# A circular-convolution and maxout kernel on one core: filter loaded in natural order and expanded by one-hot products, transposes in bf16, one group of transposes moved into the first MoE tile

## Chip, cores and metric

One core of a Trainium2 chip. The metric is the time of one execution on the device in microseconds; it is given as the median of the runs, with the lowest and highest.

## What is computed

For each of 8 sequences of 3072 tokens by 256 features, a real Fourier transform along the tokens is multiplied by a complex filter and transformed back; the result goes, token by token, through a maxout layer.

```python
X = np.fft.rfft(x, axis=1)                    # x: 8 x 3072 x 256
F = (filt_r + 1j * filt_i)[None, :, :]        # 1537 x 256
y = np.fft.irfft(X * F, n=3072, axis=1)
t = y.reshape(24576, 256)
out = np.maximum(t @ w1, t @ w2) @ w_out      # w1, w2: 256 x 1024, w_out: 1024 x 256
```

All inputs and the output are fp32; the kernel works in bf16 with fp32 sums.

## The kernel before

**The transform in stages.** 3072 tokens are 128 x 24. The forward transform is a product with the table C1 over the 128 (`f1`, or `first_s1` for batch 0), a change of layout, and a product with the table U over the 24 (px). The spectrum is multiplied by the filter F on VectorE (pq), and comes back through the tables VP and VQ (pz), a second change of layout, and the table G1 in `s4`. Batches 1 to 7 change layout by writing to DRAM and reading back (tiles ad, bt, zd, zr). Batch 0, which has nothing to hide such a trip under, does it by TensorE products with an identity (`first_t1`, `first_t2`).

**The filter tile F** has 128 partitions. A partition holds one of 12 frequency blocks, going up or going down; with padding these 24 fill a quadrant of 32. The two halves of a 64-partition group hold the same values for the real and imaginary part of X, and the two 64-partition groups hold different offsets. Before the change, `load_f` fills 12 partitions at a time, with a reversed row order for the blocks going down; `copy_f` doubles them with VectorE copies; `pad_f` writes zeros on SP; frequency 0 and the Nyquist row come by `load_f0` and `patch_f0` in fp32 and are put in by `fix_f`.

**The maxout part.** `moe_h` computes relu(t (w1 - w2)) (weights Wd), and `moe_o` adds t M with M = w2 w_out, which `prep_w` makes once. A MoE tile is 512 tokens, eight steps; there are 48 tiles.

**Order.** Each engine executes its instructions in the order in which the program emits them; there is no scheduler. The prologue (batch 0 up to `s4(0)`) is written out by hand. Then a loop over tiles and steps runs `moe_h`, `moe_o` and whatever a table `todo` holds for that step: the other batches' stages, set with `plan(step, fn, ...)`.

In the prologue's loop over eight groups g, each step does px and the products with F (`first_s2`), a t1 group two steps ahead, and pz with the Zt copy for the group before (`first_s3`). In steps 0, 2 and 4 the second half of the product with F is done on GpSimd, from a copy of px that ScalarE makes (tile xs).

**Queues and buffers.** DMAs that change the type go through POOL (GpSimd's queue): the filter, x, the weights, also the output. SP issues the rest. PSUM in the prologue is one pool `p2` of four buffers of 4 KB a partition, used in turn by every product there (pa, pt, px, pz, pg, pv, pw); afterwards it is `ps` (six of 2 KB) and `pso`.

The names used in the prediction: `xb` is x in bf16, `uu` the phases from which ScalarE's sine makes U, `At` and `Zt` the results before `first_t1` and `first_t2`, `zr` what `s4` reads, `py` the product of `s4`, `po` that of `moe_o`.

Of the kernel before, what the change touches and what calls it, by code (L numbers as in the profile page):

```python
# [8 lines left out]
FP32 = mybir.dt.float32  # L9
# [6 lines left out]
D = 256  # L16
HID = 1024
N1 = 128
N2 = 24
# [10 lines left out]
def kernel(  # L30
# [58 lines left out]
    def load_x(b, c):  # L89
        t_ = xpool.tile([128, 4, D], BF16, tag="xb", name="xb")  # L90
        src = x[b].rearrange("(p n) d -> p n d", n=N2)
        G.dma_start(out=t_, in_=src[:, 4 * c:4 * c + 4, :])  # L92
        xb[b, c] = t_


    def load_f(ri):
        f = (filt_r, filt_i)[ri]
        for c in range(2):
            src = bass.AP(f.tensor, f.offset + 16 * c * D, [[128 * D, J], [64 * D, 2], [1, 16 * D]])
            G.dma_start(out=F[64 * c:64 * c + 12, ri].rearrange("p b u d -> p b (u d)"), in_=src)  # L100
        for b in range(2):
            for c in range(2):
                row0 = 128 - 64 * b - 16 * c
                src = bass.AP(f.tensor, f.offset + row0 * D, [[128 * D, J], [-D, 16], [1, D]])
                G.dma_start(out=F[64 * c + 12:64 * c + 24, ri, b], in_=src)

    def copy_f(ri, c):
        if c == 0:
            V.tensor_copy(F[32:64, ri, :, 1:16], F[0:32, ri, :, 1:16])
        else:  # L110
            V.tensor_copy(F[96:128, ri], F[64:96, ri])

    Z0 = init.tile([8, 8 * D], BF16)
    V.memset(Z0, 0.0)

    def pad_f():
        for c in range(2):
            nc.sync.dma_start(out=F[64 * c + 24:64 * c + 32].rearrange("p r b (h u) d -> p (r b h) (u d)", h=2),
                              in_=Z0.rearrange("p (o x) -> p o x", o=1).to_broadcast([8, 8, 8 * D]))


    F0 = init.tile([64, 2, 2, D], FP32)

    def load_f0():
        for ri, f in enumerate((filt_r, filt_i)):
            for p0, n in ((0, J), (12, J), (24, 8), (32, J), (44, J), (56, 8)):
                if p0 % 32 != 12:
                    src = bass.AP(f.tensor, f.offset, [[128 * D, n], [96 * D, 2], [1, D]])
                else:
                    src = bass.AP(f.tensor, f.offset + 64 * D, [[128 * D, n], [-32 * D, 2], [1, D]])  # L130
                nc.sync.dma_start(out=F0[p0:p0 + n, ri], in_=src)

    def patch_f0():
        nc.sync.dma_start(out=F0[32:33, 1, 0], in_=filt_i[1536:1537, :])
        nc.sync.dma_start(out=F0[32:33, 0, 0], in_=filt_r[1536:1537, :])

    SW = init.tile([128, 128], BF16)
    e0 = init.tile([128, 2], FP32)
    zero = init.tile([128, 1], FP32)
    V.memset(zero, 0.0)  # L140
    pid = init.tile([128, 1], FP32)
    G.iota(pid, pattern=[[1, 1]], base=0, channel_multiplier=1,
# [14 lines left out]
    V.memset(I128, 0.0)  # L157
    V.memset(SW, 0.0)
    V.memset(U.rearrange("p t (q x) -> p t q x", q=2)[:, :, :, 24:32], 0.0)
    V.memset(VP[:, :, :, 48:64], 0.0)  # L160
    G.affine_select(out=I128, in_=I128, pattern=[[-1, 128]], compare_op=OP.not_equal,
                    fill=1.0, base=0, channel_multiplier=1)
    for c in range(2):
        for q in range(2):
            sl = SW[:, 64 * c + 32 * q:64 * c + 32 * q + 32]
            G.affine_select(out=sl, in_=sl, pattern=[[-1, 32]], compare_op=OP.not_equal,
                            fill=1.0 - 2.0 * q, base=-64 * c - 32 * (1 - q), channel_multiplier=1)


    load_f(0)  # L170
    load_f(1)
    for c in range(6):
        load_x(0, c)

# [18 lines left out]
    def tables_u():  # L193
# [53 lines left out]

        V.tensor_scalar(t1, pid, 32.0, None, OP.is_ge)
        V.tensor_scalar(t1, t1, -32.0, pid, OP.mult, OP.add)
        V.tensor_scalar(e0[:, 0:1], t1, 0.0, None, OP.is_equal)  # L250
        V.tensor_scalar(e0[:, 1:2], e0[:, 0:1], -1.0, 1.0, OP.mult, OP.add)
# [3 lines left out]
    def sines_u(uu, mk):  # L255
        Uv = U.rearrange("p t (q x) -> p t q x", q=2)
        for q in range(2):
            S.activation(U[:, :, 32 * q:32 * q + 24], uu[:, q].rearrange("p t r j -> p t (r j)"),
                         AF.Sin, bias=zero, scale=TWO_PI)
        for dr in range(2):  # L260
            S.activation(Uv[:, 0, :, 12 * dr:12 * dr + 12], uu[:, :, 0, dr], AF.Sin, bias=zero, scale=mk[:, dr:dr + 1])

# [6 lines left out]
    def tables_pe():  # L269
        pg = p2.tile([128, 128], FP32, tag="p2", name="pg")  # L270
        TE.matmul(pg, C1, I128, start=True, stop=True)
        S.activation(G1, pg, AF.Copy)
        for h in (1, 0):
            pv = p2.tile([128, 2, 8, 64], FP32, tag="p2", name="pv")
            for u in range(8):
                for c, b in QUADS:
                    TE.matmul(pv[64 * c:64 * c + 64, b, u, 0:48],
                              U[64 * b:64 * b + 48, 16 * h + 8 * (u // 4) + 4 * c + u % 4],
                              I128[64 * b:64 * b + 48, 64 * b:64 * b + 48], start=True, stop=True)
            S.activation(VP[:, 8 * h:8 * h + 8, 0, 0:48], pv[:, 0, :, 0:48], AF.Copy)  # L280
            V.tensor_copy(VP[:, 8 * h:8 * h + 8, 1, 0:48], pv[:, 1, :, 0:48])
        for h in (1, 0):
            pw = p2.tile([128, 2, 512], FP32, tag="p2", name="pw")
            for k in range(2):
                TE.matmul(pw[:, k], SW, VP[:, 8 * h + 4 * k:8 * h + 4 * k + 4], start=True, stop=True)
            E = S.activation if h else V.tensor_copy
            E(VQ[:, 8 * h:8 * h + 8].rearrange("p u b n -> p (u b n)"), pw.rearrange("p k n -> p (k n)"),
              *((AF.Copy,) if h else ()))

# [133 lines left out]
    def first_t1(g, E):  # L423
        pt = p2.tile([128, 2, 2, D], FP32, tag="p2", name="pt")
        t0 = 8 * (g // 2) + 2 * (g % 2)
        for c in range(2):
            for i in range(2):
                for dh in range(2):
                    a_ = Af[:, 3072 * dh:3072 * dh + 4096].rearrange("p (m k) -> p k m", k=64)
                    for b in range(2):  # L430
                        TE.matmul(pt[64 * b:64 * b + 64, c, i, 128 * dh:128 * dh + 128],
                                  a_[:, 2 * (t0 + 4 * c + i) + b], I128, start=True, stop=True)
        o = bt[0][0:ROWS, 8 * (g // 2):8 * (g // 2) + 8].rearrange("p (c u) d -> p c u d", c=2)[:, :, 2 * (g % 2):2 * (g % 2) + 2]
        evac(E, o, pt[0:ROWS])

# [6 lines left out]
    def first_s2(g, pool):  # L442
# [7 lines left out]
        for k in range(2):  # L450
            pq.append(pqpool.tile([128, 2, 2, D], BF16, tag="pq", name="pq"))
            E, src = V, px[:, k]
            if k == 1 and pool:
                E = G
                src = init.tile([128, 2, D], FP32, tag="xs", name="xs")
                S.activation(src[0:FROWS], px[0:FROWS, k], AF.Copy)
# [4 lines left out]

    def first_s3(g, pq, Zt):
        pz = p2.tile([128, 2, 512], FP32, tag="p2", name="pz")
# [12 lines left out]

    def first_t2(j, E, Zt):
        pt = p2.tile([128, 4, D], FP32, tag="p2", name="pt")
        for n in range(4):
            for dh in range(2):  # L480
                TE.matmul(pt[:, n, 128 * dh:128 * dh + 128], Zt[:, dh, :, 4 * j + n], I128, start=True, stop=True)
        evac(E, zr[0][:, 4 * j:4 * j + 4].rearrange("p n d -> p (n d)"), pt.rearrange("p n d -> p (n d)"))
# [62 lines left out]

    pad_f()
    load_f0()
    patch_f0()
    table_c()
    Af = init.tile([128, 7168], BF16, name="At")  # L550
    At = Af[:, 0:6144].rearrange("p (h a n k) -> p h a n k", h=2, a=2, n=N2)
# [6 lines left out]
    load_wo()  # L558
    copy_f(0, 0)
    copy_f(0, 1)  # L560
    first_s1(0)
    sines_u(uu, mk)
    Zt = init.tile([128, 2, 128, N2], BF16, tag="uz", name="Zt")
    first_s1(1)
    copy_f(1, 0)
    copy_f(1, 1)
    tables_pe()
    for c in range(2, 6):
        first_s1(c)
    fix_f()  # L570
    order = (4, 5, 6, 7, 2, 3, 1, 0)
    first_t1(4, S)
    first_t1(5, V)
    pend = None
    for n, g in enumerate(order):
        pq = first_s2(g, n in (0, 2, 4))
        if n + 2 < 8:
            first_t1(order[n + 2], S)
        if n in (1, 3, 5):
            prep_wd(n // 2, *wf)  # L580
        if pend:
            first_s3(*pend, Zt)
        pend = g, pq
    first_s3(*pend, Zt)
    zr[0] = zrpool.tile([128, N2, D], BF16, tag="zr", name="zr")
    for j in range(6):
        first_t2(j, (V, S)[j % 2], Zt)
    setup.close()
# [36 lines left out]

    plan(5, prep_w)
    plan_f1(1, spaced(0, 0.5, 12), 6)
# [61 lines left out]
```

## Time and profile before

| | us |
|---|---|
| median of 13 runs | 567.47 |
| lowest, highest | 565.84, 568.75 |
| profiled execution: time | 568.25 |
| profiled execution: span | 566.1 |
| first product on PE | 31.7 |
| first px of batch 0 | 47.24 |
| end of the last Zt copy | 71.19 |
| first py (`s4(0)`) | 77.48 |
| first po | 92.94 |

| engine | busy us | share of the span |
|---|---|---|
| PE | 504.3 | 89% |
| PEld | 349.8 | 62% |
| ACT | 335.1 | 59% |
| DVE | 322.0 | 57% |
| POOL | 82.8 | 15% |

PE is TensorE's products, PEld its weight loads (they overlap), DVE is VectorE, ACT ScalarE, POOL GpSimd, SP SyncE; POOLq and SPq are their DMA issues. A share is an average over the whole span, and the prologue and the tiles have different limits, so times of stages count for more here. The clock column of a stage is the TensorE clock granted, 1.00 being full; idle time can show as 1.00. A timeline row has start, length, engine, line, operation, output and inputs, count, and in brackets the idle time before it and what ended that.

### The profile page before, as it was taken

The numbers are of one execution on the slowest core, as the hardware profiler recorded it, in microseconds if no ns is written. First come the engines' busy times: TensorE is split into PE (matmuls) and PEld (weight loads), VectorE is DVE, ScalarE is ACT, GpSimd is POOL, SyncE is SP. The second block draws the span as 40 slices with busy tenths as digits, with TensorE's granted clock in tenths as the row PEclk, the third lists the DMA queues.
The fourth block names the chain that finished last, engine by engine and source line by source line (L and its number), as shares of the span: only waits on it lengthen the run. The fifth ranks groups of instructions, "written<-read, shape, count | busy, mean of one in ns | idle before, by whom it ended". The sixth has DMA issues, their size and how long they took to land.

```text
span 566.1 us, 12026 instructions
## 1 busy us (share of the span) xinstructions
PE 504.3 (89%) x5068; PEld 349.8 (62%) x5145; DVE 322.0 (57%) x418; ACT 335.1 (59%) x595; POOL 82.8 (15%) x133
## 2 busy tenths in 40 slices
PE   0057788999999999999999999998999999999996
PEld 0045555566666676667666766666666766677774
DVE  8354732693377447654777367733875488643432
ACT  1055667578568856785567546764667556645541
POOL 4564600110110021001100120011100000000000
PEclk9997569999999999999999999999999999999999
DMA  8998214877996797579946895759855953441111
GB/s 79 87 267 145 40 39 115 147 166 184 267 186 163 199 223 181 162 193 200 217 124 196 210 194 146 197 150 215 176 145 185 202 129 100 131 136 68 76 73 76
DMA packets 69882, 87.56 MB, mean 155 GB/s; under 512 B 4706, under 2 KB 50532, under 8 KB 68836
## 3 DMA queue, kind: packets, MB, share of 16 engines
q1 hardware_dynamic: 52052, 44.84, 37.3%
q0 software_dynamic: 17776, 41.95, 29.6%
q8 instruction: 40, 0.66, 0.5%
q14 instruction: 14, 0.11, 0.1%
HBM read 53.74 MB, written 47.19 MB: 178 GB/s over the span
## 4 chain that ended last, share of the span: by engine, by line
PE 38%; issue 27%; DMA 5%; POOL 2%; DVE 1%; ACT 0%; POOLq 0%; SPq 0%
PE po L533 14%; PE ph L508 12%; PE po L528 3%; DMA bt<-ad 3%; PE pz L378 2%; PE px L397 2%; PE pa L343 2%; DMA ad<-at 2%; PE py L492 2%; POOL out_dram L539 2%; DVE pq L402 1%; ACT at L344 0%; SPq L353 0%; POOLq L684 0%; POOL xb L92 0%
## 5 line engine op out<-in xcount | busy, mean ns | idle before, releaser
L513 ACT ACTIVATE gt<-ph 128x512 bf16<-128x512 f32 x307 | 182.2, 600 | 110.6 <-PE ph L508 108.8
L533 PE MATMUL po<-Wo,gt 128*128 128x256 bf16 x1536 | 229.8, 273 | 3.2
L533 PEld LDWEIGHTS <-gt 128*128 128x128 bf16 x1536 | 150.2, 98 | 57.6
L402 DVE TENSOR_TENSOR pq<-px,F 120x1024 bf16<-120x1024 f32 x112 | 131.7, 1218 | 24.7 <-PE px L397 24.0
L535 DVE COPY ot<-po 128x512 f32<-128x512 f32 x96 | 66.3, 690 | 110.5 <-PE po L533 109.9
L539 POOL DMA_DIRECT2D out_dram<-ot x48 | 25.8, 538 | 451.2 <-DVE ot L535 403.4
L382 ACT ACTIVATE zt<-pz 112x512 bf16<-112x512 f32 x112 | 60.8, 594 | 45.6 <-PE pz L378 40.6
L508 PEld LDWEIGHTS <-Wd 128*128 128x128 bf16 x768 | 70.3, 98 | 26.5 <-issue 12.5
L511 DVE TENSOR_SCALAR gt<-ph 128x512 bf16<-128x512 f32 x77 | 52.9, 687 | 35.8 <-PE ph L508 28.3
L344 ACT ACTIVATE at<-pa 128x512 bf16<-128x512 f32 x84 | 49.9, 603 | 8.6 <-PE pa L343 7.2
L418 PE MATMUL pa<-C,xb 128*128 128x128 bf16 x48 | 4.9, 281 | 31.9 <-DMA xb<-in_x_dram 31.9
L492 PE MATMUL py<-G,zr 128*128 128x128 bf16 x384 | 29.8, 219 | 1.9 <-ACT zr L440 1.1
L343 PE MATMUL pa<-xb,C 128*128 128x512 bf16 x83 | 31.5, 390 | 0.0
L92 POOL DMA_DIRECT2D xb<-in_x_dram x48 | 29.5, 624 | 5.0 <-PE pa L418 3.1
L378 PE MATMUL pz<-pq,VP 56*64 56x256 bf16 x448 | 28.7, 271 | 1.0 <-DVE pq L402 0.8
L492 PEld LDWEIGHTS <-zr 128*128 128x128 bf16 x384 | 24.8, 98 | 6.5 <-issue 3.3
L378 PE MATMUL pz<-pq,VQ 56*64 56x256 bf16 x448 | 28.0, 268 | 0.0
L397 PE MATMUL px<-bt,U 48*64 48x256 bf16 x448 | 23.7, 281 | 2.4 <-DMA bt<-ad 2.4
L418 PEld LDWEIGHTS <-xb 128*128 128x128 bf16 x48 | 4.4, 131 | 32.7 <-DMA xb<-in_x_dram 32.2
L420 ACT ACTIVATE At<-pa 128x1024 bf16<-128x1024 f32 x6 | 5.8, 1023 | 28.4 <-PE pa L418 28.4
L457 DVE TENSOR_TENSOR pq<-px,F 120x1024 bf16<-120x1024 f32 x13 | 15.3, 1219 | 6.0 <-PE px L447 6.0
L397 PEld LDWEIGHTS <-U 48*64 48x64 bf16 x448 | 8.3, 104 | 14.6 <-issue 11.8
(357 smaller groups left out, 575.3 us busy)
## 6 DMA issues: line engine op xcount, KB each, us to landing
out_dram<-ot POOLq DMA_DIRECT2D x48, 512.0 KB, 4.3
xb<-in_x_dram POOLq DMA_DIRECT2D x48, 256.0 KB, 7.2
ad<-at SPq DMA_DIRECT2D x42, 256.0 KB
bt<-ad SPq DMA_DIRECT2D x28, 384.0 KB
zd<-zt SPq DMA_DIRECT2D x56, 192.0 KB
zr<-zd SPq DMA_DIRECT2D x14, 768.0 KB
wf<-in_moe_w_dram POOLq DMA_DIRECT2D x2, 1024.0 KB, 7.4
F<-Z SPq DMA_DIRECT2D x2, 256.0 KB
```

The costliest lines, as they stand in the source:

```text
L343: TE.matmul(pa, C1, xb[b, c // 2][:, 2 * (c % 2):2 * (c % 2) + 2], start=True, stop=True)
L344: S.activation(at[:, 2 * (c % 2):2 * (c % 2) + 2], pa, AF.Copy)
L378: TE.matmul(pz[c][64 * k:64 * k + 64, i], W[64 * c:64 * c + 56, 2 * g + i, k], pq[k][64 * c:64 * c + 56, ri, i], start=(ri == 0), stop=(ri ...
L382: S.activation(zt[0:ROWS, c, o:o + 2], pz[c][0:ROWS], AF.Copy)
L397: TE.matmul(px[k][64 * c:64 * c + 64, i], U[64 * k:64 * k + 48, t_], bt_[64 * k:64 * k + 48, t_], start=True, stop=True)
L402: V.tensor_tensor(pq[k][0:FROWS], px[k][0:FROWS].rearrange("p (o i) d -> p o i d", o=1).to_broadcast([FROWS, 2, 2, D]), F[0:FROWS, :, k, 2 ...
L492: TE.matmul(py[:, n], zr[b][:, 4 * i + n, 128 * dc:128 * dc + 128], G1, start=True, stop=True)
L508: TE.matmul(ph, Wd[:, dc, 128 * j:128 * j + 128], y_[:, dc].rearrange("p a b -> p (a b)"), start=(dc == 0), stop=(dc == 1))
L511: V.tensor_scalar(gt[tt][:, j], ph, 0.0, None, OP.max)
L513: S.activation(gt[tt][:, j], ph, AF.Relu)
L533: TE.matmul(p_, g_[:, jj, 128 * n:128 * n + 128], Wo[:, jj], start=False, stop=(jj == 7))
L535: V.tensor_copy(ot[tt][:, n - 1:n + 1], po[tt])
```

## The change

- The filter is loaded as 96 partitions of 16 rows in natural order (`load_f`, one DMA each for the real and the imaginary part, into zr-pool buffers). Batch 0's x is issued ahead of it, and both ahead of the iotas on POOL.
- `expand_f` makes two row pairs of F at a time: 16 products with one-hot matrices Sel pick, reverse, double and place the blocks, and ScalarE copies the result from PSUM. It runs 16 times: eight for the real part and two for the imaginary part ahead of the prologue's loop, six in it. `copy_f` and `pad_f` are gone. Inside a quadrant the order of the 24 rows is changed, and U, SW, e0 and F0 with it.
- `first_t1`, `first_t2` and `tables_pe` use transposes with bf16 results instead of products with fp32 results. The eight t1 groups are now all ahead of the loop, copied by VectorE; VP is copied in one instruction.
- Of `first_t2` only group 0 stays in the prologue; groups 1 to 5 are planned at steps 0 to 4 of the tile loop. `prep_w` moves from step 5 to 7. Zt no longer shares memory with the phases; xs comes from another pool.

```diff
     def load_f(ri):
-        f = (filt_r, filt_i)[ri]
-        for c in range(2):
-            src = bass.AP(f.tensor, f.offset + 16 * c * D, [[128 * D, J], [64 * D, 2], [1, 16 * D]])
-            G.dma_start(out=F[64 * c:64 * c + 12, ri].rearrange("p b u d -> p b (u d)"), in_=src)
...
+        Fs[ri] = zrpool.tile([96, 16, D], BF16, tag="zr", name="Fs")
+        src = (filt_r, filt_i)[ri]
+        G.dma_start(out=Fs[ri], in_=src[0:1536].rearrange("(p u) d -> p u d", u=16))
+
+    def expand_f(g, ri, E):
+        pf = p2.tile([128, 2, 2, D], FP32, tag="p2", name="pf")
+        for b in range(2):
+            for i in range(2):
+                u = 2 * g + i
+                for c in range(2):
+                    for dr in range(2):
+                        m, o = 4 * b + c, u
+                        if dr:
+                            m, o = (7 - m, 16 - u) if u else (7 - m + c, 0)
+                        p0 = 64 * c + 32 * dr
+                        TE.matmul(pf[p0:p0 + 32, b, i], Sel[:, m], Fs[ri][:, o], start=True, stop=True)
+        evac(E, F[:, ri, :, 2 * g:2 * g + 2].rearrange("p b u d -> p b (u d)"), pf.rearrange("p b u d -> p b (u d)"))
...
+    for c in range(6):
+        load_x(0, c)
+    load_f(0)
+    load_f(1)
     pid = init.tile([128, 1], FP32)
     G.iota(pid, pattern=[[1, 1]], base=0, channel_multiplier=1,
...
-        pt = p2.tile([128, 4, D], FP32, tag="p2", name="pt")
+        pt = P.tile([128, 4, D], BF16, tag="p2" if P is p2 else "ps", name="pt")
         for n in range(4):
             for dh in range(2):
-                TE.matmul(pt[:, n, 128 * dh:128 * dh + 128], Zt[:, dh, :, 4 * j + n], I128, start=True, stop=True)
+                TE.transpose(pt[:, n, 128 * dh:128 * dh + 128], Zt[:, dh, :, 4 * j + n], I128)
...
-    copy_f(0, 0)
-    copy_f(0, 1)
-    first_s1(0)
+    for c in range(6):
+        first_s1(c)
     sines_u(uu, mk)
...
     order = (4, 5, 6, 7, 2, 3, 1, 0)
-    first_t1(4, S)
-    first_t1(5, V)
+    for g in order[:4]:
+        first_t1(g, V)
+    tables_pe()
+    for g in order[:4]:
+        expand_f(g, 0, S)
+    for g in order[4:]:
+        first_t1(g, V)
+    tables_q(1, S)
+    tables_q(0, V)
+    for g in order[4:]:
+        expand_f(g, 0, S)
     pend = None
+    expand_f(4, 1, S)
     for n, g in enumerate(order):
+        if n < 7:
+            expand_f(order[n + 1], 1, S)
+        if n == 6:
+            fix_f()
         pq = first_s2(g, n in (0, 2, 4))
-        if n + 2 < 8:
-            first_t1(order[n + 2], S)
...
-    for j in range(6):
-        first_t2(j, (V, S)[j % 2], Zt)
+    first_t2(0, V, p2)
...
-    plan(5, prep_w)
+    for j in range(1, 6):
+        plan(j - 1, first_t2, j, (S, V)[j % 2], ps)
+    plan(7, prep_w)
```

More of the change, by code (lines that the diff above doesn't have):

```diff
@@ L93, in load_x @@
         xb[b, c] = t_
+    Sel = init.tile([96, 8, 32], BF16)
+    Fs = {}
     def load_f(ri):
-        f = (filt_r, filt_i)[ri]
-        for c in range(2):
-            src = bass.AP(f.tensor, f.offset + 16 * c * D, [[128 * D, J], [64 * D, 2], [1, 16 * D]])
-            G.dma_start(out=F[64 * c:64 * c + 12, ri].rearrange("p b u d -> p b (u d)"), in_=src)
-        for b in range(2):
[L102 to L122, printed above, removed]
+        Fs[ri] = zrpool.tile([96, 16, D], BF16, tag="zr", name="Fs")
[3 more added lines that the diff above has]
+        pf = p2.tile([128, 2, 2, D], FP32, tag="p2", name="pf")
+        for b in range(2):
+            for i in range(2):
[8 more added lines that the diff above has]
+        evac(E, F[:, ri, :, 2 * g:2 * g + 2].rearrange("p b u d -> p b (u d)"), pf.rearrange("p b u d -> p b (u d)"))
+    F0 = zpool.tile([64, 2, 2, D], FP32, tag="zt", name="F0")
     def load_f0():
@@ L126, in load_f0 @@
             for p0, n in ((0, J), (12, J), (24, 8), (32, J), (44, J), (56, 8)):
-                if p0 % 32 != 12:
+                if p0 < 32:
                     src = bass.AP(f.tensor, f.offset, [[128 * D, n], [96 * D, 2], [1, D]])
@@ L133, in patch_f0 @@
     def patch_f0():
-        nc.sync.dma_start(out=F0[32:33, 1, 0], in_=filt_i[1536:1537, :])
-        nc.sync.dma_start(out=F0[32:33, 0, 0], in_=filt_r[1536:1537, :])
+        nc.sync.dma_start(out=F0[12:13, 1, 0], in_=filt_i[1536:1537, :])
+        nc.sync.dma_start(out=F0[12:13, 0, 0], in_=filt_r[1536:1537, :])
     SW = init.tile([128, 128], BF16)
@@ L158 @@
     V.memset(SW, 0.0)
+    V.memset(Sel, 0.0)
     V.memset(U.rearrange("p t (q x) -> p t q x", q=2)[:, :, :, 24:32], 0.0)
@@ L162 @@
                     fill=1.0, base=0, channel_multiplier=1)
[L163 to L173, printed above, removed]
+    for q in range(2):
+        sl = SW.rearrange("p (c x) -> p c x", x=32)[:, :, 12 * q:12 * q + 12]
+        G.affine_select(out=sl, in_=sl, pattern=[[-32, 4], [-1, 12]], compare_op=OP.not_equal,
+                        fill=1.0 - 2.0 * q, base=-12 * (1 - q), channel_multiplier=1)
+    sl = Sel[:, :, 0:24].rearrange("p m (q j) -> p m q j", q=2)
+    for q in range(2):
+        G.affine_select(out=sl[:, :, q], in_=sl[:, :, q], pattern=[[-1, 8], [-8, J]], compare_op=OP.not_equal,
+                        fill=1.0, base=0, channel_multiplier=1)
     def table_c():
@@ L246, in tables_u @@
         V.tensor_tensor(uu, uu, ru, OP.subtract)
-        V.tensor_scalar(t1, pid, 32.0, None, OP.is_ge)
-        V.tensor_scalar(t1, t1, -32.0, pid, OP.mult, OP.add)
-        V.tensor_scalar(e0[:, 0:1], t1, 0.0, None, OP.is_equal)
+        V.tensor_scalar(t1, pid, 12.0, None, OP.is_equal)
+        V.tensor_scalar(e0[:, 0:1], pid, 0.0, t1, OP.is_equal, OP.add)
         V.tensor_scalar(e0[:, 1:2], e0[:, 0:1], -1.0, 1.0, OP.mult, OP.add)
@@ L255, in sines_u @@
     def sines_u(uu, mk):
-        Uv = U.rearrange("p t (q x) -> p t q x", q=2)
+        Uv = U.rearrange("p t (r x) -> p t r x", r=2)
         for q in range(2):
-            S.activation(U[:, :, 32 * q:32 * q + 24], uu[:, q].rearrange("p t r j -> p t (r j)"),
-                         AF.Sin, bias=zero, scale=TWO_PI)
+            S.activation(Uv[:, :, :, 12 * q:12 * q + 12], uu[:, q], AF.Sin, bias=zero, scale=TWO_PI)
         for dr in range(2):
-            S.activation(Uv[:, 0, :, 12 * dr:12 * dr + 12], uu[:, :, 0, dr], AF.Sin, bias=zero, scale=mk[:, dr:dr + 1])
+            S.activation(Uv[:, 0, dr, 0:24].rearrange("p (q j) -> p q j", q=2), uu[:, :, 0, dr], AF.Sin, bias=zero,
+                         scale=mk[:, dr:dr + 1])
     def fix_f():
@@ L269, in tables_pe, with tables_q @@
     def tables_pe():
-        pg = p2.tile([128, 128], FP32, tag="p2", name="pg")
-        TE.matmul(pg, C1, I128, start=True, stop=True)
+        pg = p2.tile([128, 128], BF16, tag="p2", name="pg")
+        TE.transpose(pg, C1, I128)
         S.activation(G1, pg, AF.Copy)
[L273 to L288, printed above, removed]
+        pv = p2.tile([128, 2, 16, 64], BF16, tag="p2", name="pv")
+        for u in range(16):
+            for c, b in QUADS:
+                TE.transpose(pv[64 * c:64 * c + 64, b, u, 0:48],
+                             U[64 * b:64 * b + 48, 8 * (u // 4) + 4 * c + u % 4],
+                             I128[64 * b:64 * b + 48, 64 * b:64 * b + 48])
+        V.tensor_copy(VP[:, :, :, 0:48].rearrange("p u b n -> p b u n"), pv[:, :, :, 0:48])
+    def tables_q(h, E):
+        pw = p2.tile([128, 2, 512], FP32, tag="p2", name="pw")
+        for k in range(2):
+            TE.matmul(pw[:, k], SW, VP[:, 8 * h + 4 * k:8 * h + 4 * k + 4], start=True, stop=True)
+        evac(E, VQ[:, 8 * h:8 * h + 8].rearrange("p u b n -> p (u b n)"), pw.rearrange("p k n -> p (k n)"))
     def load_w():
@@ L423, in first_t1 @@
     def first_t1(g, E):
-        pt = p2.tile([128, 2, 2, D], FP32, tag="p2", name="pt")
+        pt = p2.tile([128, 2, 2, D], BF16, tag="p2", name="pt")
         t0 = 8 * (g // 2) + 2 * (g % 2)
@@ L430, in first_t1 @@
                     for b in range(2):
-                        TE.matmul(pt[64 * b:64 * b + 64, c, i, 128 * dh:128 * dh + 128],
-                                  a_[:, 2 * (t0 + 4 * c + i) + b], I128, start=True, stop=True)
+                        TE.transpose(pt[64 * b:64 * b + 64, c, i, 128 * dh:128 * dh + 128],
+                                     a_[:, 2 * (t0 + 4 * c + i) + b], I128)
         o = bt[0][0:ROWS, 8 * (g // 2):8 * (g // 2) + 8].rearrange("p (c u) d -> p c u d", c=2)[:, :, 2 * (g % 2):2 * (g % 2) + 2]
-        evac(E, o, pt[0:ROWS])
+        evac(E, o.rearrange("p c u d -> p c (u d)"), pt[0:ROWS].rearrange("p c u d -> p c (u d)"))
     def evac(E, out_, in_):
@@ L454, in first_s2 @@
                 E = G
-                src = init.tile([128, 2, D], FP32, tag="xs", name="xs")
+                src = apool.tile([128, 2, D], FP32, tag="at", name="xs")
                 S.activation(src[0:FROWS], px[0:FROWS, k], AF.Copy)
@@ L460, in first_s2, with first_s3 @@
         return pq
-    def first_s3(g, pq, Zt):
+    def first_s3(g, pq):
         pz = p2.tile([128, 2, 512], FP32, tag="p2", name="pz")
@@ L475, in first_s3, with first_t2 @@
         S.activation(z, pz[:, :, 0:384].rearrange("p c (h m) -> p c h m", h=2), AF.Copy)
-    def first_t2(j, E, Zt):
-        pt = p2.tile([128, 4, D], FP32, tag="p2", name="pt")
+    def first_t2(j, E, P):
+        pt = P.tile([128, 4, D], BF16, tag="p2" if P is p2 else "ps", name="pt")
         for n in range(4):
             for dh in range(2):
-                TE.matmul(pt[:, n, 128 * dh:128 * dh + 128], Zt[:, dh, :, 4 * j + n], I128, start=True, stop=True)
+                TE.transpose(pt[:, n, 128 * dh:128 * dh + 128], Zt[:, dh, :, 4 * j + n], I128)
         evac(E, zr[0][:, 4 * j:4 * j + 4].rearrange("p n d -> p (n d)"), pt.rearrange("p n d -> p (n d)"))
@@ L544, in drain @@
             pass
-    pad_f()
     load_f0()
@@ L549 @@
     table_c()
+    Zt = late.tile([128, 2, 128, N2], BF16, name="Zt")
     Af = init.tile([128, 7168], BF16, name="At")
@@ L558 @@
     load_wo()
-    copy_f(0, 0)
-    copy_f(0, 1)
-    first_s1(0)
+    for c in range(6):
+        first_s1(c)
     sines_u(uu, mk)
[L563 to L566, printed above, removed]
+    order = (4, 5, 6, 7, 2, 3, 1, 0)
+    for g in order[:4]:
+        first_t1(g, V)
     tables_pe()
[L568 to L571, printed above, removed]
-    first_t1(4, S)
-    first_t1(5, V)
+    for g in order[:4]:
[6 more added lines that the diff above has]
+        expand_f(g, 0, S)
     pend = None
+    expand_f(4, 1, S)
     for n, g in enumerate(order):
+        if n < 7:
+            expand_f(order[n + 1], 1, S)
+        if n == 6:
+            fix_f()
         pq = first_s2(g, n in (0, 2, 4))
-        if n + 2 < 8:
-            first_t1(order[n + 2], S)
         if n in (1, 3, 5):
@@ L581 @@
         if pend:
-            first_s3(*pend, Zt)
+            first_s3(*pend)
         pend = g, pq
-    first_s3(*pend, Zt)
+    first_s3(*pend)
     zr[0] = zrpool.tile([128, N2, D], BF16, tag="zr", name="zr")
-    for j in range(6):
-        first_t2(j, (V, S)[j % 2], Zt)
+    first_t2(0, V, p2)
     setup.close()
```

## Prediction

> **What bounds the kernel now.** I read the stages first: the busy time of each engine in the stretches that the prologue falls into (columns: stretch and length, then busy us and count of PE, PEld, DVE, ACT, POOL, then granted clock, DMA share, GB/s).
>
> ```profile
> 0.00:31.70 31.70, 0.00 (x0) 0.00 (x0) 18.17 (x60) 2.28 (x5) 16.08 (x33) 1.00 0.93 92
> 31.70:47.24 15.54, 9.99 (x148) 8.21 (x150) 6.89 (x9) 11.02 (x15) 8.75 (x10) 0.93 1.08 271
> 47.24:71.24 24.00, 18.43 (x416) 13.62 (x416) 16.34 (x14) 13.76 (x17) 14.10 (x9) 0.57 0.43 67
> 71.24:77.48 6.24, 5.13 (x49) 5.08 (x49) 3.67 (x3) 3.07 (x3) 0.00 (x0) 0.63 0.01 3
> 77.48:92.94 15.46, 12.90 (x76) 6.68 (x78) 2.08 (x3) 12.49 (x25) 0.00 (x0) 0.89 0.23 85
> 92.94:566.10 473.16, 457.86 (x4381) 316.23 (x4453) 274.82 (x331) 292.42 (x531) 43.91 (x82) 1.00 0.68 164
> ```
>
> From 92.9 us PE is busy 97% of the time: its stream sets the end, and nothing there is edited. What counts is when that stream starts. For 31.7 us PE does nothing while the DMA engines are 93% busy at only 92 GB/s. The waits of that time say why:
>
> ```profile
> PEld L418 <- DMA xb<-in_x_dram: 32.2, 2, 31.7
> POOL F L105 <- DMA F<-in_filt_r_dram: 13.0, 3, 9.9
> DVE F L109 <- DMA F<-in_filt_r_dram: 7.7, 1, 7.7
> ```
>
> The first `first_s1` matmul waits for x; x's loads are issued on POOL behind twelve filter loads, and POOL's ninth filter load waits 9.9 us for an earlier one. The timeline has the x issues at 24.84. In the loop (47.24 to 71.24) I read one pair of steps:
>
> ```profile
> 58.67 0.64 PE L447 MATMUL px<-bt,U 48*64 48x256 bf16 x8
> 59.36 1.22 DVE L457 TENSOR_TENSOR pq<-px,F 120x1024 bf16<-120x1024 f32 x1 [0.71 <-PE px L447]
> 60.68 0.60 ACT L456 ACTIVATE xs<-px 120x512 f32<-120x512 f32 x1 [1.09 <-DVE pq L457]
> 61.35 2.14 POOL L457 TENSOR_TENSOR pq<-xs,F 120x1024 bf16<-120x1024 f32 x1 [1.08 <-ACT xs L456]
> 63.54 0.61 PEld L470 LDWEIGHTS <-pq 56*128 56x128 bf16 x28 [0.46 <-POOL pq L457]
> 64.22 0.64 PE L447 MATMUL px<-bt,U 48*64 48x256 bf16 x8
> ```
>
> A chain px, DVE product, ACT copy, POOL product, pz, next px, 5.55 us for two steps; no engine is full. PE ran there at about half clock (0.57).
>
> **What the skill says.** (1) *TensorE: Matmul & The Clock Gate*, "Part 3": small-M products with outputs in different 32-column groups run at once, 2.38x for three. The trace shows it for two groups only: 16 `first_t1` products (128 rows, 64 columns) take 1.05 us, 65 ns each, at half clock. No run here has four groups with 96 rows. (2) *VectorE: DVE Perf Modes*, "Why PSUM operands drop a tier": a PSUM source allows the two-fold mode for 16-bit, none for fp32. The fp32 half agrees: 1225 ns for 1024 elements. By it a bf16 PSUM copy would take an estimated 0.7 us; not shown before. (3) *DMA: Bandwidth & Descriptors*, "Why a DMA increments its semaphore by 16 and not by 1": a load over 96 partitions uses 16 engines, over 12 fewer. The filter's 92 GB/s against the 207 to 213 of x agrees in direction. (4) The first page again, "Part 4: PE-mode transpose": transposes do not count as busy for the clock; no run here shows it yet.
>
> **Part by part.** A: to the first product of the loop (before: 48.32).
> - POOL now issues six x loads and two filter loads first: 8 x 0.59 us (the row of x's issues) = 4.7, from 0.84, so the iotas start at 5.6, not 0.84. No wait ahead of them: before, eight loads were in flight before POOL stopped. Queued behind them on POOL are the iotas and selects, and DVE's table chain waits for those: it started at 2.57, now about 6.2. Shift 3.7: C1 done at 8.8 (5.1), `uu` at 17.7, DVE free at 18.4.
> - x is 6 x 262 KB as bf16; at 210 GB/s 7.5 us, landed by about 11. The filter halves, 0.79 MB each, add 3.7 us each: about 15 and 19, before their first use. The weights and batch 1, issued later on POOL, have until 60.
> - `first_s1`: from 8.8, a first product group of 1.0, then six ACT copies of 1.0: 15.9. `first_t1` x4: 4 x 1.05, PE done at 20.1; DVE copies from 18.4, 0.7 to 1.23 each, done at 21.3 to 23.3. `sines_u` 2.5 from 17.7: 20.2. The C1 and U transposes, 1.5: 21.7.
> - Then PE's order is four expansions, four t1, pw, four expansions, two more, px. One expansion is 16 products of 256 columns: at half clock a 512-column product took 0.43, so 256 take 0.21; four at once give 16 x 0.21/4 = 0.85, say 0.9. Bounds: 0.45 at full clock, 3.4 if none overlap. PE cold: 10 x 0.9 + 4 x 1.05 + 4 x 0.43 + 1 for switches = 16, and px 0.64: first product at 38.4. PE warm, ACT binds: one G1 copy 0.26, ten F copies and one VQ at 1.02 = 11.5, after a first expansion 0.9: 34.2. I take 36.3: **-12.0** (-14.1 to -9.9).
> - Gone: DVE's F copies (8.9 us) and SP's padding writes; both lay beside the wait for x and are worth nothing alone. Transposes stream as many columns as the identity products did; I price them alike (0.8 to 1.2 of it moves A by under 1 us). The VP copies become one, 0.9 to 1.7 us, hidden under the first expansions. The F0 loads on SP stay and are needed only at step 6 of the loop.
>
> B: the loop. 22.9 us from the first product to the last Zt. The t1 groups leave PE and ACT, an expansion and its F copy take their place. But every second expansion now stands between pz and the next px, on the chain shown: 3 x (0.9 + 0.38 for the switch of shapes that the timeline has as "issue") = 3.8 cold, 2.1 warm: **+3.0**. The other expansions lie under POOL's 2.14. `fix_f` (1.09 on DVE) moves ahead of step 6's products; DVE idled 0.67 there and the late px gives the rest: 0; up to +1.1 without it.
>
> C: last Zt to first py, 6.24. Now one group of 8 transposes (0.86), a drain of 0.2 and a DVE copy of 0.75 to 1.23: 2.0 to 2.3. **-4.2**.
>
> D: tile 0 gets 40 transposes: 4.3 us at half clock, 2.2 at full, and two ACT copies of 1.02, three on DVE, which idles. ACT is busy without a pause from 79.3 to 90, so neither engine hides it whole: steps 0 to 2 cold, 3 x 0.86, then one ACT copy 1.0: **+3.5** (1.5 to 5). `prep_w` from step 5 to 7: M is wanted at step 8, so PE has less beside its 0.69 copy: **+0.3** (-0.4 to +1).
>
> Sum: -12.0 + 3.0 - 4.2 + 3.5 + 0.3 = -9.4. The profiled execution took 568.25 (span 566.1, 2.15 around it), 0.8 above the median 567.47; 568.25 - 9.4 = 558.85, less 0.8: **558.0**.
>
> **Rivals.**
> R1, PE warms up: the expansions fill the array densely from 22 on, and the clock was seen rising to 1.0 at about 48.5 after dense groups. Then A is -14.1, B +2.1, C -4.2, D +2.5: -13.7, 553.8. Against it: the loop stayed at half clock from 52 on with PE nearly always busy, and t1 now consists of transposes.
> R2, slower: the expansion's 32-column products overlap less than four-fold. PE is the bound of A, ten expansions before px and three on the loop's chain, 13 in all: it decides from 0.9 + 9.4/13 = 1.6 us an expansion. Two at once, 1.75: +11, 569; none, 3.4: +32, 590. For it: no four groups shown. Against: two groups overlap fully.
> R3, little gain: x lands late because eight big loads and SP's small ones share the engines, or tile 0 pays all 4.3 and ACT's 2.0: about -3, 564.5. For: the first filter load took 15 us to land. Against: it was of narrow loads.
> That the change does not do what it says (x still behind the filter) is excluded by POOL's order.
>
> **How the numbers follow.** Main case 0.58 (own range 555.5 to 561.5), R1 0.18, R2 0.14, R3 0.10. A difference of 0.2%, 1.1 us, is about what can be told from none. Main, R1 and most of R3 are faster: 0.84; R2 with a warmer clock or R3 at its worst could end level: 0.03; slower 0.13. Range 552.5 to 565.5: it leaves out R2 and a tail of R1.
>
> **What would show it.** First L412 product at about 9, first px at 34 to 38, expansions of 0.5 to 0.9 us for 16, loop some 26 us, first py near 64, tile 0 some 19 us to the first po, then the same 473. Wrong if an expansion takes over 1.6 us, if x lands after 15, or if the stream after tile 0 lengthens by over 2 us.

## The result and the profile after

563.40 us median of 11 runs (562.30 to 566.17) against 567.64 of the kernel before: a ratio of 0.9933, 95% interval 0.9914 to 0.9951. So 4.2 us are gained, where 9.4 were forecast. All ratios below are to the kernel before, too. The profiled execution took 564.22, its span is 562.4.

The stages of the kernel after, in the columns used before (stretch and length, busy us of PE, PEld, DVE, ACT, POOL, clock, DMA, GB/s). They are cut at the first product on PE, the first product with F, the last Zt copy, the first py, the first po and the issue of the last store:

```profile
0.00:9.22 9.22, 0.00 (x0) 0.10 (x1) 3.60 (x19) 2.28 (x5) 8.12 (x26) 1.00 0.78 142
9.22:35.56 26.34, 23.22 (x428) 20.00 (x429) 16.28 (x49) 17.73 (x22) 4.27 (x8) 0.87 1.07 241
35.56:62.46 26.90, 15.82 (x392) 9.36 (x391) 17.77 (x16) 14.76 (x18) 14.04 (x9) 0.56 0.14 22
62.46:64.37 1.91, 1.08 (x8) 0.83 (x9) 0.69 (x1) 0.00 (x0) 0.00 (x0) 0.50 0.00 0
64.37:84.33 19.96, 16.62 (x116) 10.19 (x119) 4.15 (x6) 15.39 (x29) 0.00 (x0) 0.87 0.28 96
84.33:552.81 468.48, 457.85 (x4380) 316.26 (x4453) 274.84 (x331) 291.35 (x529) 43.37 (x81) 1.00 0.68 163
552.81:562.40 9.59, 0.00 (x0) 0.00 (x0) 0.00 (x0) 0.00 (x0) 0.53 (x1) 0.57 0.14 55
```

The last two stretches of the kernel before, for comparison:

```profile
92.94:561.67 468.73, 457.86 (x4381) 316.23 (x4453) 274.82 (x331) 292.42 (x531) 43.38 (x82) 1.00 0.68 164
561.67:566.10 4.43, 0.00 (x0) 0.00 (x0) 0.00 (x0) 0.00 (x0) 0.53 (x1) 0.76 0.29 118
```

The surprise stands in the last line of each. The first po comes 8.6 us earlier and the stream up to the last store takes the same 468 us, so that store is issued 8.9 us earlier. But from its issue to the end it is now 9.6 us, not 4.4, with every engine idle. The store is not the reason: its data have landed 2.9 us after the issue in both, and SP is through at 556.1. What is late is GpSimd's DRAIN, an instruction at the end of its program. Here are its rows in the view of the program's last line (min, median and max ns, then first and last start). The longest of the three is the first: it begins with the last store's issue, and in all traces here it ends only after that store has landed. After and before:

```profile
L682 POOLq DRAIN  x3: 51/93/8873, 552.8 to 562.2; - x3
```

```profile
L684 POOLq DRAIN  x3: 51/102/3649, 561.6 to 565.8; - x3
```

It lasts 8.87 us instead of 3.65, and 5.2 of the 8.9 us are lost in it.

The waits of the first 100 us, after:

```profile
PE pa L412 <- ACT C L188: 9.2, 1, 9.2
PEld L412 <- DMA xb<-in_x_dram: 5.7, 1, 5.7
```

x is there at 5.7; PE now waits for the table C1, which was made to wait behind the DMA issues on POOL, until 9.2. And the pair of steps of the loop, after (timeline):

```profile
41.32 0.64 PE L441 MATMUL px<-bt,U 48*64 48x256 bf16 x8
42.09 1.22 DVE L451 TENSOR_TENSOR pq<-px,F 120x1024 bf16<-120x1024 f32 x1 [3.04 <-PE px L441]
...
43.34 0.60 ACT L450 ACTIVATE xs<-px 120x512 f32<-120x512 f32 x1 [0.88 <-DVE pq L451]
...
44.02 2.12 POOL L451 TENSOR_TENSOR pq<-xs,F 120x1024 bf16<-120x1024 f32 x1 [2.42 <-ACT xs L450]
...
46.20 0.61 PEld L464 LDWEIGHTS <-pq 56*128 56x128 bf16 x28 [1.88 <-POOL pq L451]
...
46.87 1.05 PE L115 MATMUL pf<-Fs,Sel 96*32 96x256 bf16 x16
...
47.85 0.64 PE L441 MATMUL px<-bt,U 48*64 48x256 bf16 x8
```

The chain is the old one with the expansion as a new link before px: 6.53 us from px to px, 0.98 more than before.

### The profile page after: what moved, and what is told of

The parts are those of the page before. It is cut to its first block, busy times and chain, and to the rows that moved or that the text cites. A ratio compares the mean times of both kernels' runs of the same rounds, so it can differ in the third digit from the quotient of the medians.

```text
span 562.4 us, 12527 instructions
## 1 busy us (share of the span) xinstructions
PE 514.6 (91%) x5324; PEld 356.7 (63%) x5401; DVE 317.3 (56%) x420; ACT 341.5 (61%) x601; POOL 70.3 (13%) x123
## 3 DMA queue, kind: packets, MB, share of 16 engines
q0 software_dynamic: 15632, 41.95, 28.2%
## 4 chain that ended last, share of the span: by engine, by line
PE 48%; issue 18%; DMA 5%; DVE 2%; POOL 1%; ACT 0%; POOLq 0%; SPq 0%
PE po L527 18%; PE ph L502 16%; PE po L522 4%; DMA bt<-ad 3%; PE pz L372 3%; PE px L391 3%; PE pa L337 2%; PE py L486 2%; DMA ad<-at 2%; DVE pq L396 1%; POOL out_dram L533 1%; ACT at L338 0%; SPq L347 0%; DVE ot L529 0%; DVE gt L505 0%
## 5 line engine op out<-in xcount | busy, mean ns | idle before, releaser
L396 DVE TENSOR_TENSOR pq<-px,F 120x1024 bf16<-120x1024 f32 x112 | 131.7, 1218 | 24.5 <-PE px L391 23.7
L486 PEld LDWEIGHTS <-zr 128*128 128x128 bf16 x384 | 25.1, 99 | 6.8 <-issue 3.4
L92 POOL DMA_DIRECT2D xb<-in_x_dram x48 | 26.2, 554 | 10.1 <-DMA Fs<-in_filt_i_dram 3.9
L391 PE MATMUL px<-bt,U 48*64 48x256 bf16 x448 | 23.7, 281 | 2.2 <-DMA bt<-ad 2.2
L434 ACT ACTIVATE F<-pf 128x1024 bf16<-128x1024 f32 x16 | 15.5, 1031 | 2.5 <-PE pf L115 2.5
L464 PE MATMUL pz<-VP,pq 56*128 56x48 bf16 x128 | 6.9, 213 | 10.2 <-POOL pq L451 6.1
L372 PEld LDWEIGHTS <-VP 56*64 56x64 bf16 x448 | 13.2, 106 | 3.1 <-DVE pq L396 1.6
```

The lines of the kernel that those rows point to most:

```text
L372: TE.matmul(pz[c][64 * k:64 * k + 64, i], W[64 * c:64 * c + 56, 2 * g + i, k], pq[k][64 * c:64 * c + 56, ri, i], start=(ri == 0), stop=(ri ...
L391: TE.matmul(px[k][64 * c:64 * c + 64, i], U[64 * k:64 * k + 48, t_], bt_[64 * k:64 * k + 48, t_], start=True, stop=True)
L396: V.tensor_tensor(pq[k][0:FROWS], px[k][0:FROWS].rearrange("p (o i) d -> p o i d", o=1).to_broadcast([FROWS, 2, 2, D]), F[0:FROWS, :, k, 2 ...
L486: TE.matmul(py[:, n], zr[b][:, 4 * i + n, 128 * dc:128 * dc + 128], G1, start=True, stop=True)
```

## The experiments

**The last drain.** GpSimd issues 101 DMAs after and 111 before, and the profile's packets on its queue are 15632 and 17776. A packet here is one contiguous piece that a DMA moves: d_desc's six loads, in four pieces a partition instead of one, add 6 x 384. The first four runs ask whether one of these counts decides it. In d_split10 (and d_split5) ten (five) late x loads are halved; in d_desc six take four packets a partition; f_fix7 leaves the DMAs as they are.

```diff
+        if 6 * b + c >= 38:            # d_split5: 43
+            for p in (0, 64):
+                G.dma_start(out=t_[p:p + 64], in_=src[p:p + 64, 4 * c:4 * c + 4, :])
```

> The changed kernel, with ten late x loads (the last four of batch 6, all of batch 7) issued as two loads of 64 partitions each: 111 POOL loads and stores as in the kernel before, instead of 101, but almost the same number of DMA packets (15632 + 160). Theory D1 (GpSimd's last drain grows with how few DMAs it has issued, whatever their size): the last drain goes from 8.87 us to about 3.65, the time falls by about 5 us to 558. Theory D2 (it depends on the number of packets in the descriptor rings, 15632 against 17776): the drain stays near 8.5, the time near 563. Theory D3 (it has to do with what is issued at the start, x ahead of the iotas): stays 8.9.

> As d_split10, with five x loads halved: 106 POOL DMAs, 15712 packets. D1, if the drain is linear in the count: about 6.3 us and a time of 561; if it is a step, 8.9 or 3.7. D2 and D3: 8.8 and 563.

```diff
+        if b == 7:
+            G.dma_start(out=t_, in_=bass.AP(x.tensor, x.offset + (b * N + 4 * c + 3) * D, [[N2 * D, 128], [-D, 4], [1, D]]))
```

> The changed kernel, with the six x loads of batch 7 reading their four rows in reverse, so that each partition takes four packets instead of one (the last batch is computed from reordered tokens): still 101 POOL DMAs, but 15632 + 2304 = 17936 packets, near the 17776 of the kernel before. D1: drain stays 8.9 us, time 563 to 564. D2: drain about 3.5, time about 558. D3: 8.9.

Measured (last drain, then time): d_desc 3.71 us, 559.55 us (ratio 0.9857, 0.9818 to 0.9897). d_split10 9.69 us, 564.03 (0.9953, 0.9939 to 0.9966); d_split5 9.28 us, 563.44. D1 fell, in direction too: more DMAs make the drain longer, by 0.082 us each. D3 fell with d_desc. D2 is right that packets decide between short and long, but not how: 160 more packets did not shorten it a little. The other kernels here with 101 DMAs and 15632 packets (f_fix7, and t2_back and x_after_f further down) have 8.87, like the kernel after.

For d_split10's 0.82 us I first blamed its 160 packets, which gives a saw tooth of 5.1 ns a packet. The next runs add packets without DMAs: some stores turn their four rows round and so write four pieces a partition.

```diff
+        rev = 6 <= tt < 7              # o_rev2: 8, o_rev9: 15, best6: 12
+        p_ = po[tt][:, 1 - n % 2 if rev else n % 2]
...
+            if rev:
+                o = bass.AP(out.tensor, out.offset + (b * N + 4 * i + 3) * D, [[N2 * D, 128], [-D, 4], [1, D]])
```

> The changed kernel, with the store of MoE tile 6 in four packets a partition instead of one (its four rows are kept in reverse on the chip and turned round by the store): 15632 + 384 = 16016 packets. So far the drain was 8.87, 9.28, 9.69 us at 15632, 15712, 15792 packets, 5.1 ns a packet, and 3.65 and 3.71 at 17776 and 17936. Theory S (a saw tooth: it grows by 5.1 ns a packet and falls to its floor where the descriptor ring wraps, somewhere between): 8.87 + 384 x 0.0051 = 10.8 us here, if the wrap lies above 16016, else about 3.7. Theory H (a hump or a step with another cause, such as the size of the packets): 8.9.

> As o_rev1 for tiles 6 and 7: 16400 packets. Theory S with a wrap at 1024 packets for each of the 16 engines, 16384: 3.7 us. Theory S with a wrap above 16400: 12.8 us. Theory H: 8.9.

> As o_rev1 for tiles 6 to 14: 15632 + 9 x 384 = 19088 packets, well past the count of the kernel before. Theory S: the tooth grows again, so the drain is longer than 3.7, by 5.1 ns for every packet past the point where it leaves the floor; if the tooth starts at 16384, (19088 - 16384) x 0.0051 = 13.9 us. Theory H: about 3.7, as at 17776 and 17936.

Measured, in one execution each: last drains of 8.87, 3.31 and 4.02 us. The tooth is refuted, and H, which had 8.9 for o_rev2, did not hold either: 384 pieces more change nothing (o_rev1), the next 384 take 5.6 us away (o_rev2), and 2688 more add 0.7. The step lies between 16016 and 16400, and what adds 0.082 us below it is the DMA, not the packet. The profile still counts 15632 packets in these runs, so the number of pieces is worked out; that GpSimd makes more of them shows in the issue of such a store, 0.75 to 0.78 us against 0.53.

If that is a rule of the queue and not of this kernel, it must work on the kernel before:

```diff
-                src = bass.AP(f.tensor, f.offset + row0 * D, [[128 * D, J], [-D, 16], [1, D]])
+                src = bass.AP(f.tensor, f.offset + (row0 - 15) * D, [[128 * D, J], [1, 16 * D]])
...
-        G.dma_start(out=Wo, in_=moe_w_out.rearrange("(c p) j -> p c j", p=128))
+        G.dma_start(out=Wo, in_=moe_w_out.rearrange("(p c) j -> p c j", p=128))
```

> The kernel before, with fewer descriptors and the same 111 DMAs on POOL: the filter's descending blocks are read in ascending order, so that a partition takes one packet of 16 rows instead of 16 of one (8 loads x 180 = 1440 fewer), and w_out is read with 8 neighbouring rows to a partition (896 fewer); both orders are wrong for the filter and for w_out, so the output isn't the reference's. 17776 - 2336 = 15440 packets. Theory R (descriptor rings that never fill are not cleared on the way, and the last drain clears them, 0.082 us for each DMA issued; past some 16400 they are cleared on the way): the drain goes from 3.65 to 9.7 us, as in d_split10 with its 111 DMAs, and the end comes 6 us later than the prologue would make it. Rival (the long drain belongs to the changed kernel's order or buffers): 3.65 us. In the prologue the narrow filter loads get shorter, so x may land some us earlier; that is read apart, from the first product.

Measured: 14960 packets (480 of 4 bytes went as well), drain 9.69 us, as in d_split10 with its 111 DMAs; 573.57 us, 1.0095 (1.0057 to 1.0134). Its last store is issued at 561.59, the kernel before's at 561.67: it is slower by the drain alone. The row of its last line:

```profile
L684 POOLq DRAIN  x3: 51/102/9691, 561.6 to 571.8; - x3
```

All together:

| kernel | POOL DMAs | pieces | last drain us |
|---|---|---|---|
| b_few | 111 | 14960 | 9.69 |
| after | 101 | 15632 | 8.87 |
| d_split5 | 106 | 15712 | 9.28 |
| d_split10 | 111 | 15792 | 9.69 |
| o_rev1 | 101 | 16016 (worked out) | 8.87 |
| o_rev2 | 101 | 16400 (worked out) | 3.31 |
| before | 111 | 17776 | 3.65 |
| d_desc | 101 | 17936 | 3.71 |
| o_rev9 | 101 | 19088 (worked out) | 4.02 |

Below some 16,400 pieces the drain is 0.082 us x DMAs + 0.6; above, it is little more than the landing of the last store.

The traces show where the rest goes. From one of the last 19 stores to the next takes the same time in all fourteen kernels, to a few hundredths of a us, with one kind of exception: in each kernel with a short drain one DMA issue comes about 2 us late (in o_rev9 it is an x load a little ahead of these stores), and in those with a long drain none does. In o_rev2 it is the last store, here with the two last stores of the kernel after below it (timeline):

```profile
547.91 0.53 POOL L538 DMA_DIRECT2D out_dram<-ot  x1 [7.29 <-DVE ot L531]
554.55 0.55 POOL L538 DMA_DIRECT2D out_dram<-ot  x1 [6.11 <-issue]
```

```profile
548.44 0.53 POOL L533 DMA_DIRECT2D out_dram<-ot  x1 [7.29 <-DVE ot L529]
552.81 0.53 POOL L533 DMA_DIRECT2D out_dram<-ot  x1 [3.83 <-DVE ot L529]
```

That is 6.64 us instead of 4.37, and "issue" says that GpSimd waited for nothing that the trace shows. In the kernel before it is the tenth store from the end, 12.83 us after the one ahead of it, where b_few has 10.54; the next store is on time again:

```profile
480.42 0.53 POOL L539 DMA_DIRECT2D out_dram<-ot  x1 [8.76 <-DVE ot L535]
493.25 0.54 POOL L539 DMA_DIRECT2D out_dram<-ot  x1 [12.30 <-DVE gt L511]
499.90 0.53 POOL L539 DMA_DIRECT2D out_dram<-ot  x1 [6.10 <-DVE ot L535]
```

A store or x load counts 144 packets (1440 for the last ten stores), so the count at the late issue can be worked out back from the end of the program:

| kernel | late DMA, from the end | pieces without it, with it | last drain us |
|---|---|---|---|
| o_rev2 | 1st, by 2.3 us | 16256, 16400 | 3.31 |
| before | 10th, by 2.3 us | 16336, 16480 | 3.65 |
| d_desc, best6, best7 | 11th, by 2.0 us | 16352, 16496 | 3.70 to 3.71 |
| o_rev9 (an x load) | 19th, by 1.8 us | 16352, 16496 | 4.02 |

All six pass one number between 16352 and 16400 at the late DMA, and the drain is the longer, the more DMAs come from that one on. (The packets of before and d_desc are the profile's, the other counts are worked out as above.) So the time is spent either once during the run, some 2 us for which mostly nobody waits, or at the end. In o_rev2 the late issue is the last store, so of the 5.6 us off its drain 2.3 are lost again. A ring of 16384 entries on this queue, whose finished DMAs are cleared when it is full, would fit each row; it is a guess, and what GpSimd does in these 2 us was not seen.

**The loop.**

```diff
-        if n == 6:
+        if n == 7:
             fix_f()
```

> The changed kernel with fix_f one step later in the prologue's loop (ahead of the products of step 7 instead of step 6). My prediction put fix_f at no cost; the trace after has it end at 56.29, with the products of step 6 behind it at 56.21, while px of step 6 was done at 55.0. Theory F1: it holds the last four products by about 1 us; moved, the first py comes 0.3 to 1.1 us earlier (64.4 to about 63.6) and the time by as much, unless the products of step 7 then wait for it as long. F2 (the products are bound by the copy of F or by DVE's total): no change of the first py. The last drain is the same 8.9 us under D1 and D2, as its DMAs are the same.

Measured: first product to last Zt 26.7 us against 26.9; 564.91 us, 0.9957 (0.9921 to 0.9993), not to be told from the kernel after. First py at 63.2, but d_split10 and d_split5, with `fix_f` unmoved, have 63.3 and 63.2. F1's gain did not come; its proviso did, that the products of step 7 wait instead. The reason is the end of VectorE's queue in the loop, after and in f_fix7 (timeline; L262 and L263 are `fix_f`):

```profile
53.17 1.94 DVE L262 TENSOR_SCALAR F<-F,e 64x256 bf16<-64x256 f32 x1
55.54 0.34 DVE L262 TENSOR_SCALAR F<-F,e 64x256 bf16<-64x256 f32 x1 [0.43 <-ACT F L434]
55.81 0.48 DVE L263 CAST F<-F 64x512 bf16<-64x512 f32 x1
56.21 4.59 DVE L451 TENSOR_TENSOR pq<-px,F 120x1024 bf16<-120x1024 f32 x4
```

```profile
54.16 2.35 DVE L451 TENSOR_TENSOR pq<-px,F 120x1024 bf16<-120x1024 f32 x2 [1.85 <-ACT Zt L469]
56.43 0.60 DVE L262 TENSOR_SCALAR F<-F,e 64x256 bf16<-64x256 f32 x2
56.95 0.41 DVE L263 CAST F<-F 64x512 bf16<-64x512 f32 x1
57.28 2.34 DVE L451 TENSOR_TENSOR pq<-px,F 120x1024 bf16<-120x1024 f32 x2
```

The last four products follow each other without a gap, and in f_fix7 `fix_f` stands among them without a gap, so VectorE is the bound there, and `fix_f` costs about its length on either side. In the kernel after, its first instruction fell into time in which VectorE was free (1.94 us long, while GpSimd made Wd from 52.62 to 54.97); the second waited for ScalarE's copy of F until 55.5, and with the cast it held the products, whose px was done at 55.0, until 56.2.

best6 is f_fix7 with six turned stores; best7 moves the expansion too:

```diff
-        if n < 7:
-            expand_f(order[n + 1], 1, S)
...
         pq = first_s2(g, n in (0, 2, 4))
+        if n < 7:
+            expand_f(order[n + 1], 1, S)
```

> As o_rev1 for tiles 6 to 11, 15632 + 6 x 384 = 17936 packets, as many as d_desc but with the reference's output, and with fix_f at step 7 of the prologue's loop. If the count alone decides the drain: 3.7 us, and a time of 558 to 559.5, 4 to 5 us under the changed kernel's 563.4 and 8 to 9 under the kernel before. If it was the loads of batch 7 rather than the count that shortened d_desc's drain: 8.9 us, 563.

> best6 with one more edit: in the prologue's loop the expansion stands behind px instead of ahead of it. In the trace after, the pairs of steps take 6.5 us from px to px instead of 5.55, 0.98 more, and the expansion ahead of px takes 1.05 of PE. Theory C (it is on the chain pz, expansion, px, as predicted): the pairs go back to about 5.55, the loop from its first product to the last Zt from 26.7 to about 23.8, the time falls by about 2.9 us from best6's 557.9 to 555. Rival (ACT's copies of F, 1.03 each, set the pace instead): less than 1 us. Drain 3.7 us.

Measured: best6 557.94 us, 0.9836 (0.9803 to 0.9870), drain 3.71. best7 555.27 us, 0.9778 (0.9745 to 0.9811), drain 3.70, and the loop as theory C has it: px of a pair starts at 38.97 and the next at 44.52, 5.55 us later. Its stages from the first product with F on:

```profile
34.18:57.92 23.74, 16.00 (x400) 9.66 (x399) 16.21 (x16) 14.46 (x18) 14.03 (x9) 0.54 0.18 27
57.92:59.84 1.92, 1.08 (x8) 0.83 (x8) 0.69 (x1) 0.00 (x1) 0.00 (x0) 0.50 0.00 0
59.84:80.41 20.57, 17.77 (x116) 10.58 (x119) 4.15 (x6) 14.89 (x28) 0.00 (x0) 0.83 0.34 103
80.41:547.76 467.35, 457.86 (x4381) 316.30 (x4453) 274.78 (x331) 291.53 (x529) 44.79 (x82) 1.00 0.68 163
547.76:552.22 4.46, 0.00 (x0) 0.00 (x0) 0.00 (x0) 0.00 (x0) 0.53 (x1) 0.91 0.29 118
```

The loop takes 23.7 us, 0.9 over the 22.9 of the kernel before, which had no `fix_f` in it, and from the last issue to the end it is 4.5 us, as there. It is the fastest version of this study, 12 us under the kernel before.

**Two parts undone.** For the transposes of z, five of whose six groups the change moved into tile 0:

```diff
+    for j in range(6):
+        first_t2(j, (V, S)[j % 2], p2)
...
-    for j in range(1, 6):
-        plan(j - 1, first_t2, j, (S, V)[j % 2], ps)
-    plan(7, prep_w)
+    plan(5, prep_w)
```

> The changed kernel with one part undone: all six groups of z transposes in the prologue again (still transposes with bf16 results) and prep_w at step 5. My prediction had this part at -4.2 + 3.5 + 0.3 = -0.4 us. From the traces it was -4.4 between the last Zt copy and the first py, and +4.5 from the first py to the first po. Theory M (moved, not saved: PE and ACT of tile 0 are both full): the time stays within 0.7 us of the changed kernel's 563.4; first py about 3 to 3.5 us later, tile 0 shorter by the same. Rival (tile 0 hides part of them): slower by 1.5 to 3 us. The last drain stays 8.9 us.

Measured: 562.53 us, 0.9922 (0.9892 to 0.9953). From the last Zt copy to the first po it takes 20.75 us (5.62 + 15.13), the kernel after 21.87. The time is 0.9 us under that of the kernel after, but the ratios, 0.9922 and 0.9933, can't be told apart. So theory M holds: the first py comes 3.7 us later and tile 0 is 4.8 shorter. What leaves the prologue is paid in tile 0; the part gains nothing, and in the traces it loses 1.1 us.

For the order of the loads:

```diff
-    for c in range(6):
-        load_x(0, c)
     load_f(0)
     load_f(1)
+    for c in range(6):
+        load_x(0, c)
```

> The changed kernel with one part undone: the two filter loads are issued ahead of batch 0's x, as in the kernel before, but in the new form. Theory O (the order alone made the gain of the prologue): x lands 7.5 us later, at 13 to 20 instead of 5.7 to 11; first_s1 ends at 21 to 22 instead of 15.9, all behind it moves by 4 to 6 us, time 568. Theory W (the new form of the loads, 96 partitions of long rows, made most of it): 1 to 3 us slower than the changed kernel, because the first product then waits for x only to about 13 and U's table isn't there before 20. Drain 8.9 us either way.

Measured: 570.42 us, 1.0058 (1.0039 to 1.0078), drain 8.87, first product at 13.54 and first product with F at 41.35, 5.8 after the kernel after (6.5 to 7.2 after the other runs with its prologue, below). Theory W's 1 to 3 us are out, and O has the size nearly right, with a time of 568. But its name, the order alone, is too much: the first product with F still comes 7.0 us earlier than the 48.32 of the kernel before. The order is about half of the prologue's gain; the other half was not taken apart further. Without x in front the rest of the change, drain included, is a loss.

## Why the prediction was right in the prologue and wrong in the sum

| step | forecast | measured |
|---|---|---|
| A, to the first product with F | -12.0 | -12.8 (48.32 to 35.56) |
| B, loop | +3.0 | +4.0 (22.87 to 26.90) |
| C, last Zt to first py | -4.2 | -4.4 (6.29 to 1.91) |
| D, tile 0 to the first po, with `prep_w` | +3.8 | +4.5 (15.46 to 19.96) |
| stream to the issue of the last store | 0 | -0.2 |
| last store to the end | 0 | +5.2 (4.4 to 9.6) |
| span | -9.4 | -3.7 |

The step that failed is the one that had no line of its own: "then the same 473". I took everything behind the first po as unedited, and with it the end of the program: a term of 0 without a reason, which measured +5.2 us (GpSimd's last drain, 3.65 to 8.87). The change replaced twelve narrow filter loads by two wide ones, 2144 packets fewer, so the count on GpSimd's queue never passed the step near 16,400, and the finished DMAs were paid for at the end instead of in mid-run; d_desc and b_few show it from both sides. "Part by part" priced the issues on POOL and never asked what they leave behind. The criterion "if the stream after tile 0 lengthens by over 2 us" did name the symptom, without a mechanism: from the first po to the end it went from 473.2 to 478.1. R3's 564.5 lies near the measured time, but by luck: its late x did not happen, and tile 0 cost only 0.7 us more than in the main case.

A: right in its steps, but partly lucky in its number. C1 was done at 9.2 (forecast 8.8), `first_s1` at 15.9 (15.9), expansions at 0.9 us at half clock and 0.49 at full (80 products in 2.44). x(0,0) was there at 5.7, where R3 had x late. R2 is out: sixteen expansion products take 0.62 to 1.05 us, the four column groups overlap, which agrees with "Part 3" of *TensorE: Matmul & The Clock Gate* in the Trainium skill.

The -12.0 was the middle between a cold and a warm PE, and PE was both: half clock from about 18.6 to 25, full from there to the first product with F. R1 was half true: from about 30.8 ACT's F copies set the pace, and other runs with the same prologue had the first product with F at 34.1 to 34.8, R1's 34.2; but its warm loop did not come (clock 0.56). Its counter-argument, that t1 consists of transposes, did not carry: in 64 of them (15.9 to 20.0) the clock fell to half at about 18.6, but through 64 more (25.1 to 29.3), behind 64 expansion products, it stayed full.

B: the chain was right (3 x 0.98 = 2.9, and best7 gives it back), its +3.0 partly luck: it lay between 3.8 cold and 2.1 warm, the loop was cold, and the link cost 0.98 there, not the 0.9 + 0.38 that the cold sum had. The term mis-sized in the loop is `fix_f`: 0 forecast, 1.1 measured, from px of step 6 to the last Zt 8.1 us instead of 7.0. I set it against VectorE's idle 0.67 before step 6 and did not see that the loop's end is bound by VectorE.

C and D: right within 0.7 us. The bf16 copy from PSUM took 0.69 us against 1.23 from fp32 for the same 1024 elements, which agrees with the two-fold mode that the skill's *VectorE: DVE Perf Modes*, "Why PSUM operands drop a tier", leaves to 16-bit data from PSUM.

## What to carry to other kernels

Add the end of the program to the stages: last DMA issue, its landing, the last instruction; if the last is long after the landing, look for the queue that is still draining. In this case fewer and wider DMAs changed what the queue had to settle at the end; count DMAs and pieces over the whole program on both sides. And before an instruction is moved into another engine's idle time, ask whether that engine is the bound a little later.

## What the runs showed of the hardware

GpSimd's last drain was 3.3 to 4.0 us in the kernels with 16,400 or more pieces on its queue, and 8.87 to 9.69 with 16,016 or fewer, 0.082 us for each DMA. Where it was short, one DMA issue had come 1.8 to 2.3 us late, the one with which the count passed a number between 16,352 and 16,400. Six stores with four pieces instead of one, which cost 0.24 us more of an idle GpSimd each, were worth some 5 us. Whether the step lies at the same number in a kernel with other DMAs, and whether fewer DMAs below it would shorten the drain as 5 and 10 more lengthened it, was not tried.
